# Two landmark transfers on one queue and three float32 key heads on the other, in a landmark-attention and feed-forward kernel

## The chip, the cores and the metric

The kernel runs on one core of a Trainium2 chip. The core has a matrix engine (TensorE; PE in the profile, with its weight loader PEld), VectorE (DVE), ScalarE (ACT), GpSimd (POOL) and a sync engine (SP) that only issues transfers. Transfers between memory and the core's buffers are issued from the sync, activation (ScalarE's) or GpSimd queue and carried out by 16 DMA engines that all queues share. A transfer that changes the type, float32 in memory to bf16 on the core, goes through GpSimd's queue; the other two queues copy bytes as they are. The metric is the device time of one execution in microseconds (us); less is better.

## What is computed

```python
def sm_attn(qq, kk, vv):
    s = scale * np.matmul(qq, kk.transpose(0, 1, 3, 2))
    s = s - np.max(s, axis=-1, keepdims=True)
    a = np.exp(s)
    a = a / (np.sum(a, axis=-1, keepdims=True) + 1e-09)
    return np.matmul(a, vv)
p_packed = sm_attn(p, k, v)
out = sm_attn(q, p_packed, p_packed)
...
h = x @ w_in
g = np.where(pos, h, np.where(neg, 0.0, (h + beta) ** 2 / (4.0 * beta)))
return (g @ w_out).astype(np.float32)
```

There are 8 batches, 8 heads, 576 tokens, a head width of 64, and 32 landmarks `p` for each head. Landmarks attend to the keys and values and give packed values; the queries then attend to these. The result, one row of 512 for each of the 4608 tokens, goes through a feed-forward layer with 2048 hidden units and a smooth, piecewise activation (`pos` is h at or above 1, `neg` at or below -1, beta is 1).

## The kernel before

The kernel works batch by batch. For each batch it needs the keys, the values and the queries with tokens on 96 partitions, the keys and queries turned (`kT`, `qT`), the landmarks turned (`pT`), and gets from them the landmark scores `sp`, their exponential `ex`, the packed values `pk` and `ppT`, the query scores `s`, their exponential `eT`, sums, logarithm and reciprocal, and a matrix `A`. The packed values times the first weight matrix are the matrix `M` (in PSUM `mp`). The hidden layer is `h` = `A` times `M`, then the activation in three steps (`x`, `t`, `hT`), then the output `o` = `hT` times the second weight matrix.

A planner in the kernel sets the order of the work. Each step has a rank, a length for each engine that may do it, the steps it depends on and the buffers it takes; the planner plays this through with its own costs, and the kernel emits the steps in the order of their planned starts. Each engine then carries out its instructions in that order, waiting on semaphores. Wherever the plan leaves TensorE free before the first output, `warm` (L788 to L791) emits matmuls on zeros, so many as the gap would hold by the plan; their number is fixed in the program.

What is loaded at the start, all of it for batch 0 unless said otherwise:

- the landmarks of batches 0 and 1, as float32, into `p_raw`: 32 partitions, 64 KB for each batch (L309), half from the sync and half from the activation queue;
- the first four key heads, as float32, into `k_raw`: 96 partitions, 144 KB for each head (L315), two heads from each of these queues, each behind the landmarks on its queue;
- key heads 4 to 7, then the values, then the queries in three parts, then the weights and later batches, through GpSimd's queue, which turns them into bf16 on the way. Between the values and the queries GpSimd also builds the identity matrix. At most eight of its transfers are planned to be under way at once.

VectorE casts both halves of `p_raw` in one instruction (L352); TensorE transposes them (L336), and VectorE and ScalarE copy the result into `pT`. The four float32 key heads are cast into `k` by two instructions, heads 0 and 1 and heads 2 and 3, each of 96 x 768 elements, in this execution on VectorE and ScalarE. TensorE transposes the eight key heads (L377), multiplies them with the landmarks (L431, `sp`), and after `ex` multiplies with the values (L481, `pk`). The queries of batch 0 are turned in three parts (heads 0, 2, 4, 6, then 1 and 3, then 5 and 7), each as it lands.

For the planner, `load_p_raw` and `load_k_raw` are one step each, of the same assumed length whatever queues they use.

Of the kernel before, what the change touches and what calls it, by code (L numbers as in the profile page):

```python
# [121 lines left out]
def kernel(  # L122
# [10 lines left out]
    nc = tc.nc  # L133
# [78 lines left out]
    p_raw = work.tile([NP, 2, H, D], f32, tag="k1", name="p_raw", bufs=1)  # L212
    p_nat = const.tile([NP, B, H, D], bf16)
    k_raw = work.tile([TP, 4, NC * D], f32, tag="q", name="k_raw", bufs=BUFS["q"])
# [49 lines left out]
    def heads(hs):  # L264
        return slice(hs[0], hs[-1] + 1, hs.step)

    def rows_of(nm, b, hs):
        return {"k": k, "q": q, "v": v}[nm][b, heads(hs)].rearrange("h (p c) d -> p h (c d)", c=NC)
# [38 lines left out]
            load(nm, b, -960 + 10 * b + n)  # L307

    def load_p_raw(e):  # L309
        for i, queue in enumerate((nc.sync, nc.scalar)):  # L310
            queue.dma_start(p_raw[:, i], p[i].rearrange("h n d -> n h d"))

    p_first = plan.add(-1000, {"SP": (1.0, 3.3, load_p_raw)})

    def load_k_raw(e):  # L315
        for i, queue in enumerate((nc.sync, nc.scalar)):
            queue.dma_start(k_raw[:, 2 * i:2 * i + 2], rows_of("k", 0, range(2 * i, 2 * i + 2)))

    k_first = plan.add(-999, {"SP": (1.0, 4.3, load_k_raw)}, behind=[p_first])
    casts = [plan.add(-30.2 + 0.1 * i, either(  # L320
        (0.5, 0.55), (0.8, 0.85), (lambda i=i: tokens("k", 0)[:, 2 * i:2 * i + 2], lambda i=i: k_raw[:, 2 * i:2 * i + 2])),
# [458 lines left out]
    for t in (t for t in order if t.engine == "PE"):  # L780
        if t.start >= first_o:
            break
        n = math.ceil((t.start - at) / 0.2135) if at < 5.0 else int((t.start - at - 0.1) / 0.1085)
# [43 lines left out]
```

## Time and profile before

| | us |
|---|---|
| median of 3 runs | 246.28 |
| lowest and highest of the 3 | 246.12 to 247.0 |
| the profiled execution | 246.44 |
| its span, first to last instruction | 244.7 |
| TensorE busy | 235.9 (96%) |
| ScalarE busy | 196.8 (80%) |
| VectorE busy | 177.0 (72%) |

Rows of the profile give the start, the length, the engine, the line, the operation with what it writes and reads, and how many were merged; a bracket says how long the engine stood idle before it and what ended that. "SPq" and "ACTq" are the issuing of a transfer on the sync or activation queue, not the transfer itself. In rows of DMA queues stand the queue, its kind, the number of packets, the MB and their share of the 16 engines' time (over 100% when packets overlap). In rows by stretch stand the stretch, its length, the busy time of PE, PEld, DVE, ACT and POOL with the number of instructions, the granted TensorE clock, the DMA share and the rate in GB/s. In rows of the queues' order a number behind a semaphore's name is cut to the same figure everywhere; DMAHW0, DMAHW1 and so on are the completion semaphores of transfers from the sync and activation queues, used in turn.

### The profile page before, as it was taken

How to read it: one execution, taken by the hardware profiler on the slowest of the kernel's cores; microseconds unless marked ns; L12 is line 12 of the kernel's file. 1: busy time of each engine (PE TensorE's matmuls, PEld its weight loads, DVE VectorE, ACT ScalarE, POOL GpSimd, SP SyncE). 2: the span in 40 equal slices, each digit the busy share in tenths (PEclk: the TensorE clock that was granted, in tenths of full speed). 3: DMA queues.
4: the chain of work that ended last, by engine and by line, in shares of the span. 5: the costliest groups of instructions: out<-in, count | busy, mean ns of one | idle time of the engine just before them, and what ended most of it. 6: DMA issues, size and time to landing. Idle time of an engine off the chain costs nothing.

```text
span 244.7 us, 5478 instructions
## 1 busy us (share of the span) xinstructions
PE 235.9 (96%) x2185; PEld 137.1 (56%) x2222; DVE 177.0 (72%) x301; ACT 196.8 (80%) x332; POOL 29.0 (12%) x42
## 2 busy tenths in 40 slices
PE   8999989999999999999999999999999999999993
PEld 2645646465545665566465546655565455555453
DVE  4548985579978996799899559948996877775000
ACT  3586988899969987998999799899978998876111
POOL 8452130000130030031003001100000000000000
PEclk9999999999999999999999999999999999999999
DMA  7999999999399999999999999967611111122223
GB/s 163 197 206 205 205 207 204 203 156 172 116 151 237 202 169 194 214 162 216 232 148 163 240 165 135 182 120 139 142 44 46 43 46 44 43 54 79 54 75 86
DMA packets 59194, 35.85 MB, mean 147 GB/s; under 512 B 31904, under 2 KB 54688, under 8 KB 59168
## 3 DMA queue, kind: packets, MB, share of 16 engines
q0 software_dynamic: 24256, 18.25, 50.6%
q1 hardware_dynamic: 34208, 16.69, 33.9%
q10 hardware_dynamic: 704, 0.56, 0.8%
q8 instruction: 17, 0.28, 0.5%
q14 instruction: 9, 0.07, 0.1%
HBM read 37.22 MB, written 9.44 MB: 191 GB/s over the span
## 4 chain that ended last, share of the span: by engine, by line
PE 85%; DVE 5%; DMA 4%; issue 3%; ACT 2%; POOL 1%; POOLq 0%
PE o L723 47%; PE h L649 24%; DMA q<-in_q_dram 4%; PE mp L529 3%; PE o L791 2%; DVE hT L670 2%; PE sp L431 2%; PE sm L561 2%; PE pk L476 1%; DVE t L663 1%; PE s L516 1%; PE tp L377 1%; DVE M L197 1%; ACT x L655 1%; PE pk L486 1%
## 5 line engine op out<-in xcount | busy, mean ns | idle before, releaser
L723 PE MATMUL o<-w_out_sb,hT 128*128 128x512 bf16 (+1 forms) x559 | 142.3, 373 | 2.1 <-issue 0.8
L670 DVE SCALAR_TENSOR_TENSOR hT<-t 128x576 bf16<-128x576 f32 (+1 forms) x130 | 94.0, 745 | 9.1 <-ACT t L665 7.0
L655 ACT ACTIVATE x<-h 128x576 f32<-128x576 f32 (+1 forms) x130 | 78.9, 654 | 7.4 <-PE h L649 5.7
L723 PEld LDWEIGHTS <-hT 128*128 128x128 bf16 x592 | 55.6, 98 | 49.0 <-issue 5.8
L649 PE MATMUL h<-A,M 128*128 128x288 bf16 x512 | 78.8, 286 | 0.3
L649 PEld LDWEIGHTS <-M 128*128 128x128 bf16 x512 | 49.5, 98 | 27.2 <-issue 0.7
L665 ACT ACTIVATE t<-x 128x576 f32<-128x576 f32 (+1 forms) x62 | 42.9, 694 | 1.0
L663 DVE TENSOR_SCALAR t<-x 128x576 f32<-128x576 f32 (+1 forms) x68 | 31.0, 456 | 10.5 <-ACT x L655 10.4
L197 ACT CAST M<-mp 128x1024 bf16<-128x1024 f32 (+1 forms) x20 | 19.1, 991 | 5.1 <-PE mp L529 5.0
L197 ACT COPY ob<-o 128x512 f32<-128x512 f32 (+1 forms) x19 | 11.0, 577 | 14.7 <-PE o L723 14.5
L197 DVE CAST M<-mp 128x1024 bf16<-128x1024 f32 (+1 forms) x14 | 15.5, 1108 | 4.1 <-PE mp L529 4.1
L575 DVE SCALAR_TENSOR_TENSOR A<-eT,rs,rc 128x576 bf16<-128x576 bf16 x16 | 12.5, 815 | 7.2 <-ACT rc L570 7.2
L197 DVE COPY ob<-o 128x512 f32<-128x512 f32 x18 | 12.4, 691 | 6.4 <-PE o L723 5.8
L274 POOL DMA_DIRECT2D k<-in_k_dram x8 | 6.2, 779 | 75.6 <-DMA kT<-k 51.9
L791 PE MATMUL o<-zeros 128*128 128x512 bf16 (+1 forms) x42 | 13.3, 435 | 1.4 <-DVE zeros L227 1.2
L437 ACT ACTIVATE ex<-sp 96x768 bf16<-96x768 f32 x16 | 12.2, 801 | 1.9 <-PE sp L431 1.9
L556 ACT ACTIVATE eT<-s,rs 128x576 bf16<-128x576 f32 x16 | 11.0, 740 | 1.5 <-PE s L516 1.3
L274 POOL DMA_DIRECT2D v<-in_v_dram x8 | 6.8, 849 | 43.1 <-DVE vv L463 37.0
L529 PE MATMUL mp<-w_in_sb,ppT 64*32 64x512 bf16 x256 | 10.7, 380 | 0.8 <-DVE M L197 0.8
L197 ACT CAST ppT<-pk 64x128 bf16<-64x128 f32 x22 | 5.7, 260 | 6.8 <-PE pk L486 6.5
L565 ACT ACTIVATE ln<-sm 128x576 f32<-128x576 f32 x16 | 10.2, 652 | 0.5
L570 ACT ACTIVATE rc<-ln 128x576 f32<-128x576 f32 x16 | 10.3, 682 | 0.1
(50 smaller groups left out, 115.4 us busy)
## 6 DMA issues: line engine op xcount, KB each, us to landing
v<-in_v_dram POOLq DMA_DIRECT2D x8, 576.0 KB, 11.4
out_dram<-ob SPq DMA_DIRECT2D x23, 192.0 KB, 3.1
k<-in_k_dram POOLq DMA_DIRECT2D x7, 576.0 KB, 7.8
q<-in_q_dram POOLq DMA_DIRECT2D x7, 576.0 KB, 14.6
out_dram<-ob SPq DMA_DIRECT2D x24, 128.0 KB, 2.4
w_out_sb<-in_moe_w_out_dram POOLq DMA_DIRECT2D x4, 512.0 KB, 19.8
w_in_sb<-in_moe_w_in_dram POOLq DMA_DIRECT2D x3, 512.0 KB, 13.9
out_dram<-ob SPq DMA_DIRECT2D x23, 64.0 KB, 2.2
```

Source lines behind the costliest of these rows:

```text
L197: i = (nc.vector.tensor_copy if e == "DVE" else nc.scalar.copy)(to, of)
L274: G_.dma_start(tokens(nm, b)[:, heads(hs)], rows_of(nm, b, hs))
L437: nc.scalar.activation(have["ex", b][:, :, 64 * i:64 * i + 64], have["sp", b, i][:TP, :E * X * G], AF.Exp, scale=scale)
L529: nc.tensor.matmul(have["mp", b, f][a * NP:(a + 1) * NP, g], have["ppT", b][r, g, a], w_in_sb[r, a, f * FW:(f + 1) * FW], start=True, stop ...
L575: V.scalar_tensor_tensor(have["A", b][:, g, xs], have["eT", b, g][:, xs], rs_of[b][:, g, :1], have["rc", b, g][:, xs], ALU.mult, ALU.mult)
L649: nc.tensor.matmul(have["h", b, fi][:, hf, :HALF], have["M", b][:, g, fi * P:(fi + 1) * P], have["A", b][:, g, hf], start=(g == 0), stop=( ...
L655: nc.scalar.activation(have["x", b, fi][:, hs[0]:hs[-1] + 1], have["h", b, fi][:, hs[0]:hs[-1] + 1, :HALF], AF.Prelu, bias=-1.0, alpha=0.5)
L663: V.tensor_scalar(t, x, 1.0, 0.0, ALU.add, ALU.max)
L665: nc.scalar.activation(t, x, AF.Relu, bias=1.0)
L670: V.scalar_tensor_tensor(dst, t, 1.0, t, ALU.min, ALU.mult)
L723: nc.tensor.matmul(have["o", key][:, :w], hT[:, fi, i * P:(i + 1) * P], w_out_sb[:, fi, cols], start=(fi == 0), stop=(fi == KF - 1))
L791: nc.tensor.matmul(o[:, :w], zeros[:, :P], zeros[:, :w], start=True, stop=True)
```

## The change

Both halves of the landmarks are issued from the sync queue. Key heads 0 and 1 are issued from the activation queue in one transfer, key head 2 from the activation queue in a second, and key head 3 from the sync queue behind the landmarks. There are five transfers instead of four, with the same bytes, sources and destinations. The lines below the two functions move down by one.

```diff
     def load_p_raw(e):
-        for i, queue in enumerate((nc.sync, nc.scalar)):
-            queue.dma_start(p_raw[:, i], p[i].rearrange("h n d -> n h d"))
+        for i in range(2):
+            nc.sync.dma_start(p_raw[:, i], p[i].rearrange("h n d -> n h d"))
 
     p_first = plan.add(-1000, {"SP": (1.0, 3.3, load_p_raw)})
 
     def load_k_raw(e):
-        for i, queue in enumerate((nc.sync, nc.scalar)):
-            queue.dma_start(k_raw[:, 2 * i:2 * i + 2], rows_of("k", 0, range(2 * i, 2 * i + 2)))
+
+        for queue, hs in ((nc.scalar, range(2)), (nc.scalar, range(2, 3)), (nc.sync, range(3, 4))):
+            queue.dma_start(k_raw[:, heads(hs)], rows_of("k", 0, hs))
 
     k_first = plan.add(-999, {"SP": (1.0, 4.3, load_k_raw)}, behind=[p_first])
```

## The prediction

> **What bounds the kernel now.** I read the page's busy shares first, then the chain that ended last, then the start of the program row by row, since all that the change touches is issued in the first 2 us. From the page:
>
> ```profile
> span 244.7 us, 5478 instructions
> PE 235.9 (96%) x2185; PEld 137.1 (56%) x2222; DVE 177.0 (72%) x301; ACT 196.8 (80%) x332; POOL 29.0 (12%) x42
> ```
>
> TensorE is busy for 96% of the span, so a start that is shorter by d ends the kernel d earlier. But the first 20 us of "busy" hold filler matmuls on zeros. What sets the start is in the chain that ended last, first 40 us:
>
> ```profile
> 4.85 8.70 DMA q<-in_q_dram
> 13.60 0.43 PE tp L377 x6
> 14.03 0.25 PE s L516 x8
> 20.32 2.07 PE h L649 x16
> ```
>
> The chain waits 8.70 us for the queries of batch 0, which GpSimd's queue fetches behind its own share of the keys and the values. Then come the last six query transposes, the scores s, and at 20.32 the first hidden layer h, after which TensorE has real work without a break. The four transfers that the change rearranges are not on this chain; their consumers' waits, in order of time:
>
> ```profile
> 0.74 0.38 SPq L311 DMA_DIRECT2D p_raw<-in_p_dram  x1
> 0.77 0.42 ACTq L311 DMA_DIRECT2D p_raw<-in_p_dram  x1
> 1.18 0.43 SPq L317 DMA_DIRECT2D k_raw<-in_k_dram  x1
> 1.22 0.48 ACTq L317 DMA_DIRECT2D k_raw<-in_k_dram  x1
> 2.09 0.79 POOL L274 DMA_DIRECT2D v<-in_v_dram  x1
> 3.31 0.69 DVE L352 CAST p_nat<-p_raw 32x1024 bf16<-32x1024 f32 x1 [0.91 <-DMA p_raw<-in_p_dram]
> 4.29 0.39 PE L336 MATMUL tpp<-ident,p_nat 32*128 32x32 bf16 x8
> 4.62 2.23 PE L791 MATMUL o<-zeros 128*128 128x512 bf16 x5
> 5.74 0.77 DVE L197 CAST k<-k_raw 96x768 bf16<-96x768 f32 x1 [0.44 <-DMA k_raw<-in_k_dram]
> 5.95 0.83 ACT L197 CAST k<-k_raw 96x768 bf16<-96x768 f32 x1 [0.49 <-DMA k_raw<-in_k_dram]
> 6.68 1.26 PE L377 MATMUL tp<-ident,k 96*128 96x96 bf16 x24
> 9.19 1.46 PE L791 MATMUL o<-zeros 128*128 128x512 bf16 x6
> 10.58 0.84 PEld L481 LDWEIGHTS <-v 96*64 96x64 bf16 x48 [0.42 <-DMA v<-in_v_dram]
> 12.73 0.28 PEld L377 LDWEIGHTS <-q 96*128 96x128 bf16 x6 [0.30 <-DMA q<-in_q_dram]
> 13.60 0.28 PEld L377 LDWEIGHTS <-q 96*128 96x128 bf16 x6 [0.50 <-DMA q<-in_q_dram]
> ```
>
> The brackets are the point. The weight loader waits 0.42 us for v, then 0.30 and 0.50 us for q: the branch through p_raw and k_raw arrives early at each of these joints. Its slack before the last q is 0.42 + 0.30 + 0.50 = 1.22 us on the loader. On VectorE and ScalarE the casts of packed values and queries stand in the same order and leave less; I take 0.5 us as what may be lost on this branch free of charge.
>
> The branch has a second effect: its bytes share the DMA engines with GpSimd's stream. DMA share and rate by stretch (last two columns; the first bytes, the landmarks', move in the first row, about 1 us after their issue), and what each queue moved in 4.10 to 5.25 and in 5.25 to 10 (q1 is sync's, q10 activation's, q0 GpSimd's):
>
> ```profile
> 1.50:2.00 0.50, 0.50 (x2) 0.15 (x1) 0.40 (x4) 0.50 (x1) 0.50 (x1) 1.00 0.29 71
> ...
> 2.50:3.00 0.50, 0.50 (x3) 0.23 (x2) 0.00 (x0) 0.00 (x0) 0.50 (x2) 1.00 0.76 164
> 3.00:3.50 0.50, 0.50 (x3) 0.18 (x2) 0.19 (x1) 0.00 (x0) 0.43 (x3) 1.00 0.85 298
> 3.50:4.00 0.50, 0.50 (x3) 0.00 (x0) 0.49 (x1) 0.00 (x0) 0.50 (x1) 1.00 1.04 332
> ```
>
> ```profile
> q0 software_dynamic: 145, 0.11, 64.1%
> q10 hardware_dynamic: 88, 0.11, 38.2%
> q1 hardware_dynamic: 36, 0.04, 11.4%
> ```
>
> ```profile
> q0 software_dynamic: 1233, 0.92, 129.0%
> ```
>
> Alone, GpSimd's queue moves 0.92 MB in 4.75 us, 0.194 MB/us. Before 4.10 it moved nothing. In the 1.15 us to 5.25 it moved 0.11 MB where it would have moved 0.223, because 0.15 MB of hardware transfers were still under way. That shortfall, 0.113 MB or 0.58 us, delays v and q by 0.58 us, and q is on the chain.
>
> **The change, part by part.** Planner costs are untouched, and TensorE, VectorE and ScalarE keep their compute order; only DMA issues and semaphore numbers move.
>
> (1) Second landmark half to sync, behind the first. It was issued at 0.77 and goes out at about 0.74 + 0.38 and a gap, at 1.18, where sync's k_raw stood: 0.41 us later. Issue to landing:
>
> ```profile
> k_raw<-in_k_dram ACTq DMA_DIRECT2D x1, 288.0 KB, 4.7
> p_raw<-in_p_dram SPq DMA_DIRECT2D x1, 64.0 KB, 2.1
> p_raw<-in_p_dram ACTq DMA_DIRECT2D x1, 64.0 KB, 2.4
> ```
>
> It landed at 0.77 + 2.4 = 3.17; now between 1.18 + 2.1 = 3.28 and 1.18 + 4.7 = 5.88 (treated like a key transfer). With 64 KB it is nearest to the landmark rows: I take 3.6, 0.4 later, since new key packets run beside it. What queues behind: the VectorE cast p_nat (3.31 to 3.7), the eight transposes at 4.29 (to 4.7), the five fillers, which are issued in order and take 0.41 us each (4.62 to 6.68), so the key transposes move from 6.68 to about 7.0. Cost 0: the 0.42 us wait for v covers it. If that cover went, 0.3 to 0.4 us of it would show.
>
> (2) Keys 0 and 1 to activation, alone in front. Issue 1.18 to 0.77, 0.41 us earlier, with no landmark before them: 288 KB. VectorE's cast of k waited 0.44 us for them; that wait goes, and what is late next is the landmark copy before it. Gain on this branch 0: the fillers and v are behind.
>
> (3) Keys 2 to activation, key 3 to sync, 144 KB each. Key 2 goes out at about 1.2, as now. Key 3 is sync's third issue, at 1.18 + 0.43 = 1.61, 0.4 us later than now. ScalarE's cast now waits for both, and stands ahead of ScalarE's copies of kT. Activation's queue carries 432 KB for 352, sync's 272 KB. Bounds for that cast's start (5.95): 0.49 earlier, its wait gone; 0.4 later, key 3's issue carried through. I take 0, since a smaller transfer makes up for the later issue. Cost 0 either way, under the slack of 0.5.
>
> (4) One more DMA, 0.4 us of issue on sync; sync's next work is a store at 45.85 us: nothing. The extra transfer moves every later hardware semaphore by one place. On sync's queue, from the start, before:
>
> ```order
> L822 UNCONDITIONAL_BRANCH [waits barrier_Pool_Activation_PE_DVE_SP_release]
> L311 DMA p_raw<-in_p_dram 32x8x64
> L317 DMA k_raw<-in_k_dram 96x2x384
> L741 DMA out_dram<-ob 96x512 [waits DVE_49]
> L741 DMA out_dram<-ob 32x512
> L406 DMA_TRANSPOSE kT<-k 128x24x96 [waits DMASW3_49,PE_49,Activation_49]
> L406 DMA_TRANSPOSE qT<-q 128x24x96 [waits DMASW1_49,PE_49,Activation_49]
> ```
>
> and after:
>
> ```order
> L823 UNCONDITIONAL_BRANCH [waits barrier_Pool_Activation_PE_DVE_SP_release]
> L311 DMA p_raw<-in_p_dram 32x8x64 x2
> L318 DMA k_raw<-in_k_dram 96x384
> L742 DMA out_dram<-ob 96x512 [waits DVE_49]
> L742 DMA out_dram<-ob 32x512
> L407 DMA_TRANSPOSE kT<-k 128x24x96 [waits DMASW3_49,PE_49,Activation_49]
> L407 DMA_TRANSPOSE qT<-q 128x24x96 [waits DMASW1_49,DMAHW0_49,PE_49,Activation_49]
> ```
>
> The first qT transpose gains a wait (DMAHW0) for a transfer of the first microseconds, done some 50 us earlier: free. On ScalarE's queue, before:
>
> ```order
> L174 ACT_TABLE_LOAD
> L311 DMA p_raw<-in_p_dram 32x8x64
> L317 DMA k_raw<-in_k_dram 96x2x384
> L197 COPY pT<-tpp 64x2x4x32 [waits DVE_49,PE_49]
> L197 COPY pT<-tpp 64x2x4x32
> L197 COPY k<-k_raw 96x768 [waits DMAHW3_49]
> ```
>
> and after:
>
> ```order
> L174 ACT_TABLE_LOAD
> L318 DMA k_raw<-in_k_dram 96x2x384
> L318 DMA k_raw<-in_k_dram 96x384
> L197 COPY pT<-tpp 64x2x4x32 [waits DVE_49,PE_49]
> L197 COPY pT<-tpp 64x2x4x32
> L197 COPY k<-k_raw 96x768 [waits DMAHW4_49,DMAHW3_49]
> ```
>
> Two issues stay two issues; the key cast now waits for two transfers.
>
> (5) Less left over at 4.10. The engines ran at 0.76 and 0.85 in 2.5 to 3.5 against 1.04 just after: (0.28 + 0.19) x 0.5 = 0.24 us of engine time unused, after the landmarks and before the keys came in full. Keys that go out 0.41 us earlier can fill it. Upper end: the whole shortfall, 0.58 us. Lower end: nothing, as by issue times 288 KB x 0.41 earlier nearly balances 144 KB x 0.43 and 64 KB x 0.41 later. I take 0.2, near the unused time. It shows in full at q, hence at s and h.
>
> Sum: 0 + 0 + 0 + 0 - 0.2 us. The profiled execution took 246.44 us against a median of 246.28; 246.24 there, 246.1 by the median.
>
> A rule that speaks against term (5): the Trainium skill, "DMA: Bandwidth & Descriptors", section "Issuing engines are not separate DMA queues", says that transfers from sync, scalar and gpsimd share the same 16 engines, so spreading them only saves issue time. By that rule the sum is 0. The trace agrees that queues share (0.11 MB instead of 0.223 beside the others), but also shows engines not full at 2.5 to 3.5, where issue time is what is missing.
>
> **Rivals.** Measurement can tell about 0.5%, 1.23 us.
>
> A: the stream gains 0.1 to 0.4 us, as summed: 245.9 to 246.2.
>
> B: the change does nothing. The later landmarks and key 3 take up what the earlier keys free: 246.2 to 246.4. For it speaks the byte balance in (5).
>
> C: the hardware queues clear before GpSimd's first packet, the whole 0.58 us comes: 245.7. Against it: 0.15 MB would have to be done in 0.24 us of unused time, at 332 GB/s 0.08 MB.
>
> D: GpSimd's stream begins earlier too. Its first transfer was issued by 2.09 and moved nothing till 4.10; landmarks moved about 1 us after issue. If it was held back by the others and not by its own preparation, up to 1 us more comes: 246.28 - 0.6 - 1.0 = 244.7, the only case over the bound on the fast side.
>
> E: the landmark's second half lands at 4.2 or later, its packets interleaved with full-rate key packets. The branch then loses 0.9 or more: 0.4 to 0.9 past the slack, 246.7 to 247.2.
>
> F, slower: TensorE's slow start lasts longer. The five fillers at 4.62 cost 0.41 us each, the six at 9.19 (9.19 to 10.58) 0.23: somewhere near 6.6 the matmuls double their rate (the granted clock column shows 1.00 throughout and doesn't tell). A longer pause ahead of the landmark transposes could put that off. At half rate the key transposes cost about 1.1 more, 24 score matmuls some 0.7, six fillers 1.1: 2.9, less 0.5 of slack, 2.4 at most. Over 1.7 us of it decides for slower; taking two thirds, 1.9 less 0.5 is 1.4: 247.7.
>
> The Trainium skill ("TensorE: Matmul & The Clock Gate", "What's actually happening") has full clock follow about 3.4 us of sustained work, in windows that run free of the kernel. Here TensorE worked from 1.19 to about 6.6 first; no row shows what pause would break a window.
>
> **How the numbers follow.** A 0.42, B 0.22, C 0.10, D 0.06, E 0.08, F 0.12. Faster is D, 0.06; slower F, 0.12; the rest within, 0.82. The likeliest is A, 246.1, its own range 245.9 to 246.2. The range takes in C below and E above, with 0.2 to 0.3 for the spread of the three runs (246.12 to 247.0): 245.4 to 247.3; D and F, 0.18, are left out.
>
> **What would show it.** Right: the landmark cast near 3.7 and its transposes near 4.7; key transposes by 7.1; the weight loader still waiting for v at about 10.4; the last q transposes near 13.4 and h about 0.2 us before 20.3; more than 0.11 MB on GpSimd's queue in 4.10 to 5.25. Wrong: no wait for v left, or a wait for kT or ex ahead of pk (E); fillers after 9 us still 0.4 us apart (F); GpSimd's first packets well before 4 us (D).

## The result, and the profile after

The changed kernel takes 248.21 us (median of 5 runs, 247.88 to 248.63), the kernel before 246.38 (median of 5, 246.12 to 247.08). The ratio is 1.0073, 95% interval 1.0056 to 1.0090: slower by 1.8 us, where 246.1 us, no measurable change, and a range of 245.4 to 247.3 were forecast. The profiled execution took 248.63 us, 2.19 more than that of before; it is the slowest of the five. In the experiments, one execution of the key part alone fell in the slow state (351.73 us, granted clock 0.66) and is left out of its median.

The page's first lines, and the largest early pieces of the chain that ended last:

```profile
span 246.9 us, 5519 instructions
PE 239.4 (97%) x2222; PEld 138.6 (56%) x2222; DVE 177.2 (72%) x301; ACT 196.9 (80%) x332; POOL 28.5 (12%) x42
```

```profile
1.18 4.04 DMA p_raw<-in_p_dram
6.45 2.24 PE o L792 x5
8.69 1.92 PE tp L378 x24
12.12 1.51 PE o L792 x7
19.96 2.26 PE o L792 x10
22.56 2.07 PE h L650 x16
```

Before, the start hung on the queries. Now it hangs on the second half of the landmarks, 4.04 us from issue, and on the filler matmuls and key transposes queued behind it on TensorE. The rows in order of time:

```profile
0.74 0.87 SPq L311 DMA_DIRECT2D p_raw<-in_p_dram  x2
0.77 0.92 ACTq L318 DMA_DIRECT2D k_raw<-in_k_dram  x2
5.32 0.68 DVE L353 CAST p_nat<-p_raw 32x1024 bf16<-32x1024 f32 x1 [2.92 <-DMA p_raw<-in_p_dram]
6.05 0.39 PE L337 MATMUL tpp<-ident,p_nat 32*128 32x32 bf16 x8 [1.69 <-DVE p_nat L353]
6.38 2.31 PE L792 MATMUL o<-zeros 128*128 128x512 bf16 x5
8.48 2.13 PE L378 MATMUL tp<-ident,k 96*128 96x96 bf16 x24
13.55 0.84 PEld L482 LDWEIGHTS <-v 96*64 96x64 bf16 x48 [0.42 <-issue]
13.56 0.94 PE L482 MATMUL pk<-ex,v 96*64 96x32 bf16 x48
16.21 0.32 PE L517 MATMUL s<-qT,ppT 64*32 64x288 bf16 x8
22.50 2.13 PE L650 MATMUL h<-A,M 128*128 128x288 bf16 x16
```

Against before: the landmark transposes are 1.76 us later (6.05 for 4.29), the key transposes 1.80 (8.48 for 6.68) and 2.13 us long instead of 1.26; pk is 2.98 later, h 2.25. The rest of the program runs as before, 2.19 us later. Of the lateness at pk, 0.73 us disappears before h (2.98 - 2.25).

What sync's queue (q1) and activation's (q10) moved from 2.40 to 3.20, when the second landmark half should have gone through:

```profile
q10 hardware_dynamic: 156, 0.22, 81.1%
q1 hardware_dynamic: 84, 0.02, 11.4%
```

Activation moved 156 packets of keys, sync 84 packets, 0.02 MB. Cut finer, sync moved 11 in 2.40 to 2.60, none in 2.60 to 2.80, 13 in 2.80 to 3.00 and 60 in 3.00 to 3.20: the second half hardly moved before 3.0. The first half, issued at 0.74, still landed after 2.2 us, so the loss is all in the second.

### The profile page after: what moved, and what is told of

Read it like the earlier page. It is cut to its first block, busy times and chain, and to the rows that moved or that the text cites. A ratio compares the mean times of both kernels' runs of the same rounds, so it can differ in the third digit from the quotient of the medians.

```text
span 246.9 us, 5519 instructions
## 1 busy us (share of the span) xinstructions
PE 239.4 (97%) x2222; PEld 138.6 (56%) x2222; DVE 177.2 (72%) x301; ACT 196.9 (80%) x332; POOL 28.5 (12%) x42
## 4 chain that ended last, share of the span: by engine, by line
PE 89%; DVE 6%; DMA 2%; ACT 1%; issue 0%; SPq 0%; DVEq 0%
PE o L724 48%; PE h L650 23%; PE o L792 4%; PE mp L530 3%; DVE hT L671 3%; PE sp L432 3%; PE tp L378 2%; PE pk L477 2%; DMA p_raw<-in_p_dram 2%; PE sm L562 2%; DVE t L664 1%; PE s L517 1%; PE pk L487 1%; DVE M L197 1%; PE pk L482 1%; DVE pT L197 0%
## 5 line engine op out<-in xcount | busy, mean ns | idle before, releaser
L724 PE MATMUL o<-w_out_sb,hT 128*128 128x512 bf16 (+1 forms) x592 | 147.5, 374 | 0.1
L792 PE MATMUL o<-zeros 128*128 128x512 bf16 (+1 forms) x46 | 14.2, 434 | 1.2 <-DVE zeros L227 1.2
```

Source lines behind the costliest of these rows:

```text
L724: nc.tensor.matmul(have["o", key][:, :w], hT[:, fi, i * P:(i + 1) * P], w_out_sb[:, fi, cols], start=(fi == 0), stop=(fi == KF - 1))
L792: nc.tensor.matmul(o[:, :w], zeros[:, :P], zeros[:, :w], start=True, stop=True)
```

## Experiments

Medians below stand against those of before on the same chip, 246.12 to 246.25. Four questions: which part of the edit, why the landing is late, whether lateness or TensorE's rate carries the loss, and whether the later transfers add to it.

**The landmark part alone.**

```diff
-        for i, queue in enumerate((nc.sync, nc.scalar)):
-            queue.dma_start(p_raw[:, i], ...)
+        for i in range(2):
+            nc.sync.dma_start(p_raw[:, i], ...)
```

> Before with the landmark part of the change alone: both halves on sync; the keys as before, two heads behind them on sync, two on activation. If the landmark order carries the loss, the second half lands about 4 us after its issue again (2.4 before), its cast starts at 4.8 to 5.4 (3.31 before) and the time is 247.6 to 248.3. If the loss comes from splitting the keys, it is 246.2 to 246.6.

Measured 248.26 us, ratio 1.0081 (1.0064 to 1.0098). The second half landed 3.7 us after issue and the cast started at 4.96:

```profile
4.96 0.68 DVE L352 CAST p_nat<-p_raw 32x1024 bf16<-32x1024 f32 x1 [2.56 <-DMA p_raw<-in_p_dram]
```

By the median, this half of the edit alone gives the whole loss, as the landmark reading expected. But it also puts sync's two key heads behind two landmark transfers, and the profiled execution, at 250.86 us the slowest of the five, was held by these keys and not by the landmarks:

```profile
8.58 0.56 DVE L197 CAST k<-k_raw 96x768 bf16<-96x768 f32 x1 [1.88 <-DMA k_raw<-in_k_dram]
9.20 2.10 PE L377 MATMUL tp<-ident,k 96*128 96x96 bf16 x24 [0.86 <-DVE k L197]
```

What the keys cost in the other four executions (247.88 to 248.36) is not shown, so this run alone does not prove that late landmarks are the cause.

**The key part alone.**

```diff
-        for i, queue in enumerate((nc.sync, nc.scalar)):
-            queue.dma_start(k_raw[:, 2 * i:2 * i + 2], ...)
+        for queue, hs in ((nc.scalar, range(2)), (nc.scalar, range(2, 3)), (nc.sync, range(3, 4))):
+            queue.dma_start(k_raw[:, heads(hs)], rows_of("k", 0, hs))
```

> Before with the key part alone: one landmark half on each queue as before; behind them keys 0 and 1, then key 2 on activation, key 3 on sync. If the landmark order carries the loss, the landmark cast starts at 3.2 to 3.5 and the time is 246.1 to 246.7. If the loss comes from the longer activation queue, the key casts start after 6.4 and the time is over 247.

Measured 246.79 us (median of nine), ratio 1.0059 (1.0024 to 1.0094), but in two groups: five runs at 246.36 to 246.79, four at 247.96 to 249.58. The profiled execution is of the lower group (246.44):

```profile
3.25 0.77 DVE L352 CAST p_nat<-p_raw 32x1024 bf16<-32x1024 f32 x1 [0.85 <-DMA p_raw<-in_p_dram]
6.53 0.83 ACT L197 CAST k<-k_raw 96x768 bf16<-96x768 f32 x1 [1.07 <-DMA k_raw<-in_k_dram]
7.41 1.11 PE L377 MATMUL tp<-ident,k 96*128 96x96 bf16 x22 [1.02 <-ACT k L197]
```

The landmarks are on time; ScalarE's cast waits 0.6 us longer for keys 2 and 3 than before (6.53 for 5.95), and TensorE pauses 1.02 us inside the key transposes. The key split gains nothing, and in some executions costs; both readings were half right. No execution of the upper group was profiled. Three of its four mean granted clocks (0.983, 0.990, 0.993) lie below all of the lower group (0.997 to 1.000), so TensorE's rate is a likely difference, but that is not shown.

**No key packets beside the landmarks.** Both halves on sync, all four key heads behind them on sync, activation's queue empty.

```diff
-        for queue, hs in ((nc.scalar, range(2)), (nc.scalar, range(2, 3)), (nc.sync, range(3, 4))):
+        for queue, hs in ((nc.sync, range(2)), (nc.sync, range(2, 4))):
```

> Both landmark halves on sync, and behind them on sync the keys in two transfers of two heads; activation's queue carries nothing, so no key packets run beside the landmarks. Theory one, the key packets on the other queue hold the second half up: it lands 2.1 to 2.6 us after its issue at 1.18 and the cast starts at 3.3 to 3.8. Theory two, the second transfer on a queue is late whatever runs beside it: 4 us after issue, cast at 5.2. The keys come later than before on one queue, so the whole may be 246.3 to 247.5 under theory one, about 248 or more under theory two.

The second half landed 2.6 us after its issue; the cast row, and sync's queue from 2.40 to 3.20:

```profile
3.87 0.73 DVE L352 CAST p_nat<-p_raw 32x1024 bf16<-32x1024 f32 x1 [1.47 <-DMA p_raw<-in_p_dram]
8.16 0.83 ACT L197 CAST k<-k_raw 96x768 bf16<-96x768 f32 x1 [2.33 <-DMA k_raw<-in_k_dram]
```

```profile
q1 hardware_dynamic: 268, 0.10, 84.5%
```

Theory one on the landing (the cast 0.07 us over its window): against 2.1 and 2.4 us before, the second place on the queue costs some 0.2 to 0.5 us; the key packets on the other queue cost the remaining 1.4 (4.04 against 2.6). The whole took 249.53 us, ratio 1.0147 (1.0128 to 1.0166), more than expected, since keys 2 and 3 now came at 8.16.

**One landmark transfer of 128 KB.**

```diff
-        for i in range(2):
-            nc.sync.dma_start(p_raw[:, i], p[i].rearrange("h n d -> n h d"))
+        nc.sync.dma_start(p_raw.rearrange("n b h d -> n (b h) d"), p[:2].rearrange("b h n d -> n (b h) d"))
```

> The changed kernel with both landmark halves in one transfer of 128 KB on sync instead of two of 64 KB; keys as in the changed kernel. If the second half was late because a second transfer had to be prepared beside two key transfers, the one transfer lands by 3.6 and the cast starts at 3.3 to 3.9: 246.0 to 246.8. If it was late because its small packets take turns with key packets on each DMA engine, the cast starts at 4.5 to 5.3 and the time is 247.5 to 248.5.

Measured 247.91 us, ratio 1.0059 (1.0039 to 1.0078). It landed 4.1 us after issue, cast at 4.88. From 2.40 to 3.20:

```profile
q10 hardware_dynamic: 116, 0.18, 68.2%
q1 hardware_dynamic: 128, 0.03, 17.7%
```

So the landmarks are late without a second issue too. 128 landmark packets went out beside 116 key packets: near enough one for one, six times the bytes on the keys' side. The Trainium skill, "DMA: Bandwidth & Descriptors", section "Queues, rings and completion order", says that a DMA engine takes turns between its queues by packet. The counts of this run agree, if the rows of 256 and 1536 bytes that the profile counts are its packets; those of the changed kernel (84 beside 156, none in 2.60 to 2.80) do not.

**Key packets of 256 bytes.** A direct test of turns: `k_raw` laid out by tokens, so that a key head comes in rows of 64 values; beside it the same transfers with rows of 384.

```diff
-    k_raw = work.tile([TP, 4, NC * D], f32, ...)
+    k_raw = work.tile([TP, NC, 4, D], f32, ...)
...
+        for queue, h in ((nc.scalar, 0), (nc.scalar, 1), (nc.scalar, 2), (nc.sync, 3)):
+            queue.dma_start(k_raw[:, :, h], k[0, h].rearrange("(p c) d -> p c d", c=NC))
```

> The changed kernel with k_raw laid out as tokens, then heads, so that each float32 key head comes in rows of 64 values (256 bytes, as the landmarks) and not of 384 (1536 bytes); heads 0, 1 and 2 in three transfers on activation, head 3 on sync behind the landmarks. If landmark and key packets take turns one by one, a turn is now short and the landmarks land earlier: cast at 3.7 to 4.6 instead of 5.32 (the keys later, as there are six times as many packets). If the queues share by bytes or the second landmark transfer waits for all keys issued before it, the cast stays at 5 or later.

> The same three key transfers on activation and one on sync, in the layout of the changed kernel, packets of 1536 bytes: the comparison for the run with small packets. Cast at 4.8 to 5.5, time 247.6 to 248.6.

Small packets: landed 3.1 us after issue, cast at 4.38 (252.67 us, ratio 1.0261, 1.0240 to 1.0282, since keys 2 and 3 were cast only at 11.28). Large ones, cut into one transfer for each head: 3.4, cast at 4.63, earlier than expected, but the time, 249.40 us (ratio 1.0114, 1.0062 to 1.0165), is longer than expected, with keys 2 and 3 cast at 8.10. The pair differs by 0.3 us, less than landings with large packets differ among the runs (3.4 to 4.4). With large packets sync moved 279 packets from 2.40 to 3.20 beside 137 of activation, two for one. Turn-taking by packet is therefore not shown to be the cause: the counts speak for it in one run and against it in two. That key traffic on the other queue is the cause is shown by the run without it; how it delays the landmarks stays open.

**A bridge over TensorE's pause, in the changed kernel.** More fillers ahead of the landmark transposes keep TensorE at work while the landmarks are late. The count that the edit raises is in half-width matmuls, so the group went from 7 to 9 full-width fillers, not to 11 as the expectation has it, and the pause from 1.69 to 0.73 us.

```diff
+    fill[0] = (fill[0][0], fill[0][1] + 4)
```

> The changed kernel with four more filler matmuls in the first group (11 for 7), so that TensorE has no pause of 1.7 us before the landmark transposes at 6.05; nothing else changes, the landmarks are as late. If the pause put off TensorE's full rate, the 24 key transposes take about 1.1 us less and h starts near 21.3 instead of 22.5: 247.0 to 247.5. If the late landing alone carries the loss, the key transposes still take about 2.1 us and the time stays at 248.0 to 248.5.

Measured 247.42 us, ratio 1.0064 (1.0042 to 1.0087):

```profile
6.24 1.25 PE L794 MATMUL o<-zeros 128*128 128x512 bf16 x5
7.84 1.27 PE L378 MATMUL tp<-ident,k 96*128 96x96 bf16 x24 [0.35 <-DVE k L197]
14.31 0.28 PEld L378 LDWEIGHTS <-q 96*128 96x128 bf16 x6 [0.52 <-DMA q<-in_q_dram]
```

The same five fillers take 1.25 us instead of 2.31: full rate. In the profiled executions h comes 1.54 us earlier (20.96 for 22.50). By the medians the bridge is worth 0.8 us (248.21 - 247.42), or 0.5 when each is set against before on its own chip (1.83 and 1.30); the intervals of the two ratios overlap, so its worth in time is not settled. The last row shows that the queries are waited for again.

**Bridged over in full**: the same line with `+ 12`, 13 fillers.

> The changed kernel with thirteen fillers in the first group. Nine of them (in the run before with a bridge) halved the pause and gave 247.4. If half rate was the cost and what is left is the later queries, the time stays at 246.8 to 247.4 and h starts at 20.7 to 21.2. If lateness still counts with TensorE busy throughout, it is 247.5 or more; if full bridging removes all, 246.5 or less.

Measured 247.61 us, ratio 1.0059 (1.0044 to 1.0074): no better. In this execution the second half landed later still, 4.4 us after issue, and a pause of 0.72 us was left, as with nine fillers; pk started at 12.63 and h at 21.57. Lateness counts at full rate too.

**One landmark transfer, bridged**: 12 fillers.

```diff
+    fill[0] = (fill[0][0], fill[0][1] + 10)
```

> The kernel with one landmark transfer and the split keys, and twelve filler matmuls in the first group instead of seven, so that TensorE works until the landmarks are there at about 5.6. Without these fillers it took 247.9, with h at 21.7 and the queries landing 8.0 us after issue (8.5 before). If TensorE's half rate was what cost, the key transposes take 1.3 us, the branch comes in before the queries, h starts at 19.8 to 20.4 and the time is 245.6 to 246.4. If the lateness costs at full rate too, h starts after 21 and the time is 247 or more.

Measured 246.88 us, ratio 1.0034 (1.0020 to 1.0048), h at 20.67: between the two readings. The bridge is worth 1.0 us here (247.91 - 246.88), and no variant beat the kernel before.

**The pause alone, landmarks on time.** In the kernel before, first 5 fillers (the expectation says 3, by the same slip), then 3, instead of 7:

```diff
+    fill[0] = (fill[0][0], fill[0][1] - 4)
```

> The kernel before with four fillers fewer in the first group (3 for 7): all transfers as before, landmarks on time, but TensorE pauses some 1.7 us ahead of the landmark transposes at 4.29. If such a pause by itself puts off TensorE's full rate, the 24 key transposes at 6.7 take about 2.1 us instead of 1.26 and the time is 246.7 to 247.8. If it needs the late landmarks, nothing moves: 246.0 to 246.5.

> The kernel before with three fillers in the first group instead of seven: the landmarks on time, TensorE idle some 1.8 us ahead of the landmark transposes, as long as after the change. (With five fillers the key transposes took 1.88 us for 1.26, and the time did not move.) If a pause costs only where the branch is late as well, 246.2 to 246.7, with pk at 11 to 12 us. If a longer pause alone can carry the loss, pk starts after 12.5 and the time is 247 to 248.

Five fillers: 246.45 us, ratio 1.0013 (0.9993 to 1.0034). Three (`- 8`): 246.74, ratio 1.0030 (1.0005 to 1.0054), runs from 246.08 to 248.94. The profiled execution with three:

```profile
4.08 0.39 PE L336 MATMUL tpp<-ident,p_nat 32*128 32x32 bf16 x8 [1.42 <-DVE p_nat L352]
6.51 2.22 PE L377 MATMUL tp<-ident,k 96*128 96x96 bf16 x24
11.36 0.94 PE L481 MATMUL pk<-ex,v 96*64 96x32 bf16 x48
20.30 2.13 PE L649 MATMUL h<-A,M 128*128 128x288 bf16 x16
```

The key transposes run at half rate, pk is 0.78 us late, h 0.05. In this execution a pause alone is nearly all absorbed. Two of the ten with three fillers, at 248.24 and 248.94, and one of the ten with five, at 248.66, were not profiled; that a pause alone cost time in these is not ruled out.

**Late landmarks, transfers untouched.** A memset on VectorE ahead of the landmark cast, in the kernel before.

```diff
         V.memset(ones2[:, 1:], 1.0 / scale)
+        V.memset(hT[:, :6].rearrange("p k t -> p (k t)"), 0.0)
```

> The kernel before with one extra memset of about 3 us on VectorE ahead of the landmark cast (of a tile that is written later anyway): all transfers as before, the cast moves from 3.31 to about 5.3, as late as in the changed kernel. If the lateness with its pause carries the loss, h starts at 21.5 to 22.5 and the time is 247.2 to 248.2. If the loss is in the transfers (the queries landed 0.6 to 0.8 us later after the change), it is 246.2 to 246.8.

> The same with four more fillers in the first group, so that TensorE does not pause while the landmarks are late. If lateness up to 2 us is absorbed once TensorE runs at full rate, h starts at 20.2 to 20.6 and the time is 246.0 to 246.6. If lateness costs by itself, 247 or more.

Measured 249.17 us, ratio 1.0104 (1.0081 to 1.0126): the cast came at 5.91, later than meant, and h at 23.03. With 9 fillers, which left a pause of 1.38 us: 248.66, ratio 1.0099 (1.0065 to 1.0133). Full rate came and went again (five fillers in 1.25 us, then 22 key transposes in 1.94), so the condition of the expectation of 246.0 to 246.6, full rate throughout, was not met, and the next run tests it. A shorter memset (`hT[:, :4]`) with 12 fillers:

> The kernel before with a memset of about 2 us on VectorE ahead of the landmark cast, and twelve fillers in the first group: transfers as before, the cast near 5.1, TensorE busy until then. If lateness of this size is nearly absorbed at full rate, pk starts at 11.3 to 12, h at 20.2 to 20.9 and the time is 246.1 to 246.8. If lateness costs whatever the rate, h starts after 21.3: 247.2 or more.

Measured 247.26 us, ratio 1.0046 (1.0031 to 1.0061), at full rate, h at 21.03; the fillers overran and put the landmark transposes at 6.29, 2.0 us late. Lateness without half rate costs 1.0 us: two microseconds are not absorbed.

**The lateness of the change, and nothing else**: `hT[:, :5]`, fillers as before.

> The kernel before with a memset of about 2.45 us on VectorE ahead of the landmark cast, fillers as before: all transfers as before, the landmark transposes as late as after the change (about 6.05). If lateness and the pause that it makes are the whole cause, h starts at 22.0 to 22.8 and the time is 247.9 to 248.6. If part of the loss is in the transfers, it is under 247.7.

Measured 247.87 us, ratio 1.0063 (1.0043 to 1.0083); four runs at 247.86 to 248.32, one at 246.91, which is the profiled one:

```profile
6.00 0.36 PE L337 MATMUL tpp<-ident,p_nat 32*128 32x32 bf16 x8 [1.63 <-DVE p_nat L353]
6.29 1.25 PE L792 MATMUL o<-zeros 128*128 128x512 bf16 x5
7.89 1.27 PE L378 MATMUL tp<-ident,k 96*128 96x96 bf16 x24 [0.35 <-DVE k L197]
20.73 2.13 PE L650 MATMUL h<-A,M 128*128 128x288 bf16 x16
```

With no transfer touched, the landmark transposes at 6.00 give the changed kernel's time within 0.4 us. So lateness and what it does to TensorE are nearly the whole cause. This execution, after a pause of 1.63 us, had full rate all the same and lost only 0.48 us at h. The other four were not profiled. Two of them have a mean granted clock of 0.993, that of the profiled execution with the late cast and nine fillers, where full rate came and went; the other two, at 0.999 and 0.997, leave it open. That all four had half rate is likely but not shown.

**The slack, from the profiled executions.** Start of the landmark transposes, pk and h, us:

| | transposes | pk | h | pk to h |
|---|---|---|---|---|
| before | 4.29 | 10.58 | 20.25 | 9.67 |
| changed | 6.05 | 13.56 | 22.50 | 8.94 |
| changed, nine fillers | 5.95 | 11.74 | 20.96 | 9.22 |
| one transfer, bridged | 5.93 | 11.73 | 20.67 | 8.94 |
| changed, thirteen fillers | 6.57 | 12.63 | 21.57 | 8.94 |
| before, three fillers | 4.08 | 11.36 | 20.30 | 8.94 |
| late cast | 6.59 | 14.09 | 23.03 | 8.94 |
| late at full rate | 6.29 | 12.09 | 21.03 | 8.94 |
| same lateness | 6.00 | 11.79 | 20.73 | 8.94 |

Once the branch through landmarks and keys ends last, pk to h is 8.94 us; before it was 9.67, the queries ending last. The branch has 0.73 us of slack, and past it every microsecond at pk is one at h. With nine fillers it is 9.22: there the queries, which landed 9.1 to 9.5 us after issue (8.4 to 8.7 before), ended last again, 0.28 us behind the branch. So the later queries add nothing in the changed kernel (8.94), and 0.28 us here, where the branch is faster. For the changed kernel: 1.76 late at the transposes, 1.22 more by half rate (2.98 at pk), less 0.73 is 2.25 at h, and 2.19 in the time.

## Why the prediction was wrong, step by step

- **What bounds the kernel**: right for before. That the branch beside the queries has slack was right; 0.5 us was taken, 0.73 measured. The 1.22 us added up on the weight loader was too much, since the first of its three waits is no slack (next point).
- **(1), the second landmark half**: the step that failed. It was bounded by 3.28 and 5.88 and put at 3.6, as nearest to the landmark rows; it landed at 5.22 (1.18 + 4.04). Those rows were taken while both queues carried landmarks and the keys had not come in. The row of the opposite end, a key transfer among key packets, described the new neighbours. The cover named, 0.42 us of waiting for v, was no cover: in the changed kernel the loader stands idle for the same 0.42 us ahead of pk, with v landed long before (its row names no transfer), while the fillers ahead of pk still run. At full rate the way from the landmark transposes to pk takes 5.79 to 5.80 us in four executions of the table (nine fillers, one transfer bridged, late at full rate, same lateness), however late it starts. The landing was put 1.62 us too early, and the cost taken as 0 became the 2.25 us at h that are added up above.
- **(2) and (3), the keys**: that they gain nothing was right, since the casts waited for the landmark copies instead. The split made alone put the cast of keys 2 and 3 0.6 us later, past the bound of 0.4; in the profiled execution the slack still covered that (h at 20.16), and whether it is what lengthened four of the others is not shown.
- **(4), semaphores and issue**: right; nothing of it shows.
- **(5), GpSimd's stream 0.2 us earlier**: its sign came, 0.13 MB instead of 0.11 in 4.10 to 5.25, but from 5.25 to 10 the queue moved 0.86 MB instead of 0.92, and the queries were no earlier. Issue to landing of the queries was 8.4 to 8.7 us before and 9.0 to 9.5 after; over runs of other variants it went from 7.9 to 10.6, and in runs whose transfers were those of before from 7.9 to 8.8. A gain of 0.2 can't be told in that, and it would not count while the landmarks end last.
- **The rivals**: E (late landmarks, 0.08) and F (full rate later, 0.12) came true together, F as a consequence of E. Their prices were near: E put 0.4 to 0.9 us past the slack, and lateness alone measured 0.5 to 1.0; F's most was 2.9 at half rate, of which 1.22 came, beyond the five fillers that ran at half rate before as well. Counting them as separate cases, each small, hid that the one opens the pause that brings the other. B's argument, bytes in balance, was beside the point: the total was not what changed.

The rule quoted against (5), from the Trainium skill, "DMA: Bandwidth & Descriptors", section "Issuing engines are not separate DMA queues", that spreading transfers saves issue time alone, gave a sum of 0. No gain was seen, which agrees, but the result was a loss of 1.8 us, which came from which transfers share the engines at the same time.

## What to carry to other kernels

In this kernel the small transfer that gates a chain of engines landed late where a large transfer was under way on another queue. Such a transfer should go out while the other queues are quiet; its landing time in a quiet moment is no price for it beside one. Where TensorE is kept busy by a fixed number of fillers, price lateness of the next real work twice, once as delay and once as a pause that may leave the matmuls behind it at half rate. A table of two events over several variants, here pk and h, gives the slack of a branch better than adding up the waits of one profile.

## What was not expected of the hardware

- Where both landmark halves go out from sync, the second, 64 KB in rows of 256 bytes, landed 2.6 us after issue without key packets on the other queue (one run), and 3.4 to 4.4 us with them (the changed kernel and four variants). The first half landed after 2.2 to 3.0 us in the same five.
- The rate of TensorE after the same pause varied: a pause of 1.63 us left full rate in one execution, one of 1.69 us half rate until about 12 us in another. The Trainium skill, "TensorE: Matmul & The Clock Gate", "What's actually happening", has the rate set by windows that run free of the kernel; the scatter in runs with a pause (246.08 to 248.94 with three fillers, 246.91 to 248.32 with the same lateness) agrees. So does a pair without any pause: the kernel before and the key part alone run the same matmuls up to 4.6 us, and their next five fillers take 2.23 and 1.25 us.
- The granted clock in the profile reads 1.00 in the first microseconds even at half rate, because the trace's records of it begin only with the first full clock (6.64 us in the kernel before, 11.94 in the changed one) and the time ahead of them counts as full. Over the 17 profiled executions this first record begins at 4.43 to 6.64 us in the seven with a pause of at most 0.73 us ahead of the landmark transposes. In the ten with a pause of 0.78 to 2.23 us it begins at 8.20 to 17.16 in eight and at 4.95 and 5.24 in two. Where full rate is lost again, the column (third from the end) does show it, here with the late cast and nine fillers:

```profile
5.24:8.65 3.41, 1.81 (x16) 0.79 (x16) 2.42 (x5) 1.57 (x3) 3.22 (x5) 1.00 1.29 193
8.65:12.06 3.41, 3.41 (x48) 3.32 (x49) 1.73 (x3) 1.73 (x3) 0.90 (x2) 0.50 1.31 201
```
